# k^T v as pairs of 64-row matmuls, with v cast whole, in a linear-attention and mixture-of-experts kernel

## The chip, the cores and the metric

The kernel runs on one core of one Trainium2 chip. The metric is the device time of one execution in microseconds (us); less is better. "Span" is the time from the first to the last instruction of the profiled execution; it is about 1.8 us shorter than the device time of the same execution. Engines: PE (TensorE matmul), PEld (its weight loads), DVE (VectorE), ACT (ScalarE), POOL (GpSimd), SP (SyncE, which here only starts loads).

## The reference

Linear attention over q, k, v of 8 batches x 8 heads x 576 positions x 64, then a mixture of 8 experts in which every token goes through every expert, weighted by eight Sinkhorn rounds:

```python
q_p, k_p = phi(q), phi(k)                       # phi(x) = elu(x) + 1
kv  = np.einsum('bhsd,bhse->bhde', k_p, v)      # k^T v: what the change is about
z   = np.sum(k_p, axis=2)
num = np.einsum('bhsd,bhde->bhse', q_p, kv)
den = np.einsum('bhsd,bhd->bhs', q_p, z)[..., None] + 1e-06
x   = num / den                                 # then 4608 tokens x 512
for e in range(8):                              # P: gate, exp, Sinkhorn
    out += P[:, e:e+1] * (np.maximum(x @ w1[e], 0) @ w2[e])
```

## The kernel before

The attention part works on 16 groups of four heads. A group's k, q and v stand on 128 partitions: two "hh" halves of 64 partitions each hold different heads and share the matmuls. For k^T v that would mix heads of both halves, so v was cast into a tile of twice the width in which each half's columns are zero on the other half's partitions. The zeros were set once; each group's cast (float32 to float16 on POOL) wrote the two halves separately:

```python
vv_t = [fp.tile([P, 2, NJ, 2, D + 1], FP16, ...) for i in range(2)]   # zeroed at the start; column D is 1 (for z)
for hh in range(2):
    def f_v(e, hh=hh):
        s = slice(64 * hh, 64 * hh + 64)
        copy(e, gvv["tile"][s, :, :, hh, 0:D], gin["v"]["tile"][s])   # 64 partitions, 1152 elements each
    tvv.append(fadd({"pool": 1.35, "dve": 0.75} if n < 2 else ("pool", 1.35), f_v, ...))

def f_kv(_):
    gkv["tile"] = aps.tile([P, 2, 2, D + 1], FP32, tag="att", name="kv_ps")
    for j in range(NJ):                                               # NJ = 9
        nc.tensor.matmul(gkv["tile"], lhsT=gt["k"]["tile"][:, j, :, :].rearrange("p r d -> p (r d)"),
                         rhs=gvv["tile"][:, :, j, :, :], start=(j == 0), stop=(j == NJ - 1))
for rr in range(2):
    def f_z(e, rr=rr):                                                # PSUM to SBUF: kvz
        s = slice(64 * rr, 64 * rr + 64)
        copy(e, gz["tile"][s, :, rr, :], gkv["tile"][s, rr, :, :])
```

phi of k and q costs DVE three passes over SBUF, and these matter later:

```python
nc.vector.tensor_scalar(out=o, in0=gin[nm]["tile"], scalar1=1.0, ..., op0=ALU.add)            # tk, tq (or on ACT)
nc.vector.tensor_scalar(out=ge["tile"], in0=ge["tile"], scalar1=1.0, ..., op0=ALU.min)        # ek, eq
nc.vector.tensor_tensor(out=o, in0=o, in1=ge["tile"], op=ALU.max)                             # tk, tq: two SBUF inputs
```

After kv come q transposes (qt), den, num, the division (rden, xn), transposes of x (xt), and then the experts' matmuls hq and ye. All attention results in PSUM share one pool of two buffers (tag "att"). The order of every engine's queue is not written by hand: a small list scheduler (`_Plan`) places each piece on its engine by assumed durations (the numbers in `fadd`), priorities and the two-deep pools. A changed duration or pool therefore changes every queue.

The softmax here doesn't subtract the row's maximum and nothing guards it: scores larger than these inputs give would overflow.

## Time and profile before

| | before |
|---|---|
| device time, median of 4 runs | 1053.62 us (1052.89 to 1054.81) |
| profiled span | 1053.3 us |
| PE busy in the span | 1012.7 us (96%) |
| first expert matmul (hq) starts | 44.08 us |
| last attention tile gone | about 168 us |
| POOL casts of v | 32, 40.2 us in all |

How to read it: PE is the bound from the moment it can start on hq, so the time is made of three things: when hq starts, how much PE work follows it, and how long PE stands idle after it. The lines are in the prediction.

### The profile page before, as it was taken

The numbers are of one execution on the slowest core, as the hardware profiler recorded it, in microseconds if no ns is written. First come the engines' busy times: TensorE is split into PE (matmuls) and PEld (weight loads), VectorE is DVE, ScalarE is ACT, GpSimd is POOL, SyncE is SP. The second block draws the span as 40 slices with busy tenths as digits, with TensorE's granted clock in tenths as the row PEclk, the third lists the DMA queues.
The fourth block names the chain that finished last, engine by engine and source line by source line (L and its number), as shares of the span: only waits on it lengthen the run. The fifth ranks groups of instructions, "written<-read, shape, count | busy, mean of one in ns | idle before, by whom it ended". The sixth has DMA issues, their size and how long they took to land.

```text
span 1053.3 us, 17028 instructions
## 1 busy us (share of the span) xinstructions
PE 1012.7 (96%) x7048; PEld 652.9 (62%) x7048; DVE 730.2 (69%) x1507; ACT 432.1 (41%) x693; POOL 54.8 (5%) x55
## 2 busy tenths in 40 slices
PE   2799999999999999999999999999999999999997
PEld 1455565456666666666666666666666666666664
DVE  6787876847666766667666766677666766666666
ACT  4666664453333333333333333333333333333331
POOL 3332310000000000000000000000000000000000
PEclk9999999999999999999999999999999999999999
DMA  9969600050001300050002200050003100014333
GB/s 270 326 193 248 198 6 2 1 81 2 1 1 26 56 1 1 1 81 1 1 1 41 41 1 1 1 81 1 1 1 49 32 2 1 1 28 89 83 82 81
DMA packets 31966, 55.63 MB, mean 53 GB/s; under 512 B 2704, under 2 KB 10896, under 8 KB 31888
## 3 DMA queue, kind: packets, MB, share of 16 engines
q1 hardware_dynamic: 18816, 37.76, 12.1%
q0 software_dynamic: 13072, 16.79, 9.9%
q8 instruction: 55, 0.90, 0.4%
q14 instruction: 23, 0.19, 0.1%
HBM read 61.88 MB, written 9.44 MB: 68 GB/s over the span
## 4 chain that ended last, share of the span: by engine, by line
PE 88%; DVE 7%; DMA 2%; ACT 1%; issue 1%; POOL 0%; SPq 0%; DVEq 0%; POOLq 0%; ACTq 0%
PE hq L467 45%; PE ye L576 36%; PE ye L497 4%; DMA vin<-in_v_dram 1%; DMA kin<-in_k_dram 1%; PE kv_ps L261 1%; DVE tk L239 1%; DVE xn L329 1%; DVE tq L239 1%; PE xt_ps L340 1%; PE qt_ps L286 1%; PE num_ps L324 0%; DVE ek L237 0%; DVE gs L389 0%; DVE kvz L195 0%
## 5 line engine op out<-in xcount | busy, mean ns | idle before, releaser
L471 ACT ACTIVATE h<-hq 128x512 f16<-128x512 f32 x576 | 343.4, 597 | 552.0 <-PE hq L467 551.8
L467 PE MATMUL hq<-xT,w 128*128 128x512 f16 x2304 | 556.2, 379 | 0.6 <-ACT h L471 0.6
L587 DVE SCALAR_TENSOR_TENSOR acc<-ye,P_sb,acc 128x256 f32<-128x256 f32 x882 | 396.7, 483 | 144.4 <-PE ye L576 144.4
L467 PEld LDWEIGHTS <-w 128*128 128x128 f16 x2304 | 223.9, 98 | 197.1 <-issue 1.9
L576 PEld LDWEIGHTS <-S 128*128 128x128 f16 x2016 | 197.0, 98 | 51.4 <-DVE S L550 2.2
L576 PE MATMUL ye<-T,S 128*128 128x256 f16 x1512 | 196.0, 273 | 1.2 <-DVE S L550 1.2
L576 PEld LDWEIGHTS <-h 128*128 128x128 f16 x1512 | 147.9, 98 | 58.1 <-ACT h L471 0.6
L550 DVE TENSOR_TENSOR S<-h 128x1024 f16<-128x1024 f16 x126 | 86.8, 689 | 115.4 <-ACT h L471 115.4
L576 PE MATMUL ye<-w,h 128*128 128x256 f16 x1008 | 130.8, 273 | 0.4 <-ACT h L471 0.4
L497 PE MATMUL ye<-w,h 128*128 128x512 f16 x288 | 69.7, 385 | 0.0
L576 PE MATMUL ye<-w,S 128*128 128x256 f16 x504 | 65.3, 273 | 0.2 <-DVE S L550 0.2
L576 PE MATMUL ye<-T,h 128*128 128x256 f16 x504 | 65.3, 273 | 0.1
L181 POOL DMA_DIRECT2D w<-in_moe_w_dram x16 | 13.3, 830 | 659.6 <-PE hq L467 624.3
L197 POOL CAST vv<-vin 64x1152 f16<-64x1152 f32 x32 | 40.2, 1257 | 98.7 <-PE kv_ps L261 49.5
L497 PEld LDWEIGHTS <-h 128*128 128x128 f16 x288 | 27.1, 100 | 27.5 <-issue 2.2
L550 DVE TENSOR_TENSOR S<-h,S 128x1024 f16<-128x1024 f16 x63 | 43.2, 686 | 0.0
L550 DVE TENSOR_TENSOR S<-S,h 128x1024 f16<-128x1024 f16 x63 | 42.9, 681 | 0.0
L261 PE MATMUL kv_ps<-vv,tk 128*128 128x260 f16 x144 | 22.5, 309 | 7.4 <-DVE qpT L195 5.0
L329 DVE TENSOR_TENSOR xn<-num_ps,rden 128x512 f16<-128x512 f32 (+1 forms) x48 | 26.5, 596 | 2.7 <-PE num_ps L324 1.9
L286 PE MATMUL qt_ps<-ident,tq 128*128 128x128 f16 x144 | 13.7, 235 | 14.1 <-DVE tq L239 11.0
L324 PE MATMUL num_ps<-kvz,qpT 128*128 128x128 f16 x160 | 16.0, 229 | 9.2 <-DVE xn L329 6.6
L226 ACT ACTIVATE ek<-kin 128x1152 f16<-128x1152 f32 x16 | 18.6, 1162 | 14.5 <-DMA kin<-in_k_dram 10.6
(60 smaller groups left out, 330.9 us busy)
## 6 DMA issues: line engine op xcount, KB each, us to landing
w<-in_moe_w_dram POOLq DMA_DIRECT2D x16, 1024.0 KB, 9.5
kin<-in_k_dram SPq DMA_DIRECT2D x16, 576.0 KB, 5.3
qin<-in_q_dram SPq DMA_DIRECT2D x16, 576.0 KB, 5.5
vin<-in_v_dram SPq DMA_DIRECT2D x16, 576.0 KB, 5.9
out_dram<-acc SPq DMA_DIRECT2D x72, 128.0 KB, 2.4
wg_sb<-in_moe_w_gate_dram POOLq DMA_DIRECT2D x1, 8.0 KB, 15.7
```

Source lines behind the costliest of these rows:

```text
L197: nc.gpsimd.tensor_copy(out=dst, in_=src)
L226: nc.scalar.activation(out=ge["tile"], in_=gin[nm]["tile"], func=AF.Exp)
L239: nc.vector.tensor_tensor(out=o, in0=o, in1=ge["tile"], op=ALU.max)
L261: nc.tensor.matmul(gkv["tile"], lhsT=gt["k"]["tile"][:, j, :, :].rearrange("p r d -> p (r d)"), rhs=gvv["tile"][:, :, j, :, :], start=(j = ...
L286: nc.tensor.transpose(gp["tile"][:, j - j0, :, :].rearrange("p h w -> p (h w)"), gt["q"]["tile"][:, j, :, :].rearrange("p r d -> p (r d)") ...
L329: nc.vector.tensor_tensor(out=gxn["tile"][:, i0:i1], in0=gn["tile"][:, 0:i1 - i0].rearrange("p i r h e -> p i (r h) e"), in1=grd["tile"][: ...
L467: nc.tensor.matmul(ghq["tile"], lhsT=gw1["tile"][:, c, ts(f, P)], rhs=xT[c][:, ds(512 * g, 512)], start=(c == 0), stop=(c == NDT - 1))
L471: nc.scalar.activation(out=gh["tile"][:, f, :], in_=ghq["tile"], func=AF.Relu)
L497: nc.tensor.matmul(gy[tt]["tile"], lhsT=gh["tile"][:, f, ds(P * tt, P)], rhs=gw2["tile"][:, f, :], start=(f == 0), stop=(f == NFT - 1))
L550: nc.vector.tensor_tensor(out=Sx[:, i], in0=a0, in1=a1, op=op)
L576: nc.tensor.matmul(g_["tile"][:, col, :], lhsT=lhs(kk), rhs=rhs(kk), start=(first and kk == 0), stop=(kk == 3), skip_group_check=True)
L587: nc.vector.scalar_tensor_tensor(out=dst, in0=g_["tile"][:, col, :], scalar=P_sb[:, gg, e:e + 1], in1=dst, op0=ALU.mult, op1=ALU.add)
```

## The change

The intent: multiply the two halves side by side on the two row halves of the PE array, each into its own PSUM bank, so that no zeros are needed. v is then cast once, whole, into a tile of half the width, and PE streams 130 columns per pair where it streamed 260. The rest follows: two "att" buffers at once per kv group, four smaller PSUM copies for two, smaller memsets, and a scheduler that can grant two buffers of one pool to one piece. The diff is abridged: it leaves out that repair of the scheduler and the dependencies that came with it (kv now waits for its kvz tile to be granted, the q transposes and num for the tiles that their results go into). They are a part of what is called "the order" below.

```diff
-    vv_t = [fp.tile([P, 2, NJ, 2, D + 1], FP16, ...
+    vv_t = [fp.tile([P, 2, NJ, D + 1], FP16, ...
...
-        for hh in range(2):
-            def f_v(e, hh=hh):
-                s = slice(64 * hh, 64 * hh + 64)
-                copy(e, gvv["tile"][s, :, :, hh, 0:D], gin["v"]["tile"][s])
-            tvv.append(fadd({"pool": 1.35, "dve": 0.75} if n < 2 else ("pool", 1.35), f_v, ...
+        def f_v(e):
+            copy(e, gvv["tile"][:, :, :, 0:D], gin["v"]["tile"])
+        tvv.append(fadd({"pool": 1.3, "dve": 0.75} if n < 2 else ("pool", 1.3), f_v, ...
-        gkv, gz = S_.grp(p_att), S_.grp(p_kvz)
+        gkv, gz = [S_.grp(p_att), S_.grp(p_att)], S_.grp(p_kvz)
...
-            gkv["tile"] = aps.tile([P, 2, 2, D + 1], FP32, tag="att", name="kv_ps")
+            for hh in range(2):
+                gkv[hh]["tile"] = aps.tile([P, 2, D + 1], FP32, tag="att", name=f"kv_ps{hh}")
             for j in range(NJ):
-                nc.tensor.matmul(gkv["tile"], lhsT=gt["k"]["tile"][:, j, :, :]...,
-                                 rhs=gvv["tile"][:, :, j, :, :], start=(j == 0), stop=(j == NJ - 1))
+                for hh in range(2):
+                    s = slice(64 * hh, 64 * hh + 64)
+                    nc.tensor.matmul(gkv[hh]["tile"], lhsT=gt["k"]["tile"][s, j, :, :]...,
+                                     rhs=gvv["tile"][s, :, j, :], start=(j == 0), stop=(j == NJ - 1))
...
-            tz.append(fadd({"dve": 0.29, "act": 0.3}, f_z, ...      # one copy per rr
+                tz.append(fadd({"dve": 0.22, "act": 0.24}, f_z, ... # one copy per hh and rr
...
-        nc.vector.memset(vv_t[i], 0.0)
-        for hh in range(2):
-            nc.vector.memset(vv_t[i][64 * hh:64 * hh + 64, :, :, hh, D], 1.0)
+        nc.vector.memset(vv_t[i][:, :, :, D], 1.0)
```

More of the change, by code (lines that the diff above doesn't have):

```diff
@@ L59, in slot @@
             r = t["ready"]
+            seen = {}
             for g in t["acq"]:
                 o, n = g["pool"]["order"], g["pool"]["n"]
-                if len(o) >= n:
-                    for u in o[len(o) - n]["users"]:
+                i = len(o) + seen.get(id(o), 0)
+                seen[id(o)] = i + 1 - len(o)
+                if i >= n:
+                    for u in o[i - n]["users"]:
                         d = self.t[u]["done"]
@@ L163 @@
     fp = front.enter_context(tc.tile_pool(name="fp", bufs=2))
-    vv_t = [fp.tile([P, 2, NJ, 2, D + 1], FP16, tag=f"vv{i}", name=f"vv{i}", bufs=1) for i in range(2)]
+    vv_t = [fp.tile([P, 2, NJ, D + 1], FP16, tag=f"vv{i}", name=f"vv{i}", bufs=1) for i in range(2)]
     kvz_t = [fp.tile([P, 2, 2, D + 1], FP16, tag=f"kvz{i}", name=f"kvz{i}", bufs=1) for i in range(2)]
@@ L249, in att @@
         ta = fadd(("none", 0.0), f_va, deps=[tin["v"]], acq=[gvv], prio=pr)
-        for hh in range(2):
-            def f_v(e, hh=hh):
-                s = slice(64 * hh, 64 * hh + 64)
-                copy(e, gvv["tile"][s, :, :, hh, 0:D], gin["v"]["tile"][s])
-            tvv.append(fadd({"pool": 1.35, "dve": 0.75} if n < 2 else ("pool", 1.35), f_v, deps=[ta, tin["v"]],
-                            use=[gvv, gin["v"]], prio=pr))
-        gkv, gz = S_.grp(p_att), S_.grp(p_kvz)
+        def f_v(e):
+            copy(e, gvv["tile"][:, :, :, 0:D], gin["v"]["tile"])
@@ L258, in f_kv @@
+        tvv.append(fadd({"pool": 1.3, "dve": 0.75} if n < 2 else ("pool", 1.3), f_v, deps=[ta, tin["v"]],
+                        use=[gvv, gin["v"]], prio=pr))
+        gkv, gz = [S_.grp(p_att), S_.grp(p_att)], S_.grp(p_kvz)
         def f_kv(_):
-            gkv["tile"] = aps.tile([P, 2, 2, D + 1], FP32, tag="att", name="kv_ps")
+            for hh in range(2):
+                gkv[hh]["tile"] = aps.tile([P, 2, D + 1], FP32, tag="att", name=f"kv_ps{hh}")
             for j in range(NJ):
-                nc.tensor.matmul(gkv["tile"], lhsT=gt["k"]["tile"][:, j, :, :].rearrange("p r d -> p (r d)"),
-                                 rhs=gvv["tile"][:, :, j, :, :], start=(j == 0), stop=(j == NJ - 1))
@@ L263, in att @@
-        tkv = fadd(("pe", 1.0), f_kv, deps=[tph["k"]] + tvv, acq=[gkv], use=[gvv, gt["k"]], prio=pr)
+                for hh in range(2):
+                    s = slice(64 * hh, 64 * hh + 64)
+                    nc.tensor.matmul(gkv[hh]["tile"], lhsT=gt["k"]["tile"][s, j, :, :].rearrange("p r d -> p (r d)"),
+                                     rhs=gvv["tile"][s, :, j, :], start=(j == 0), stop=(j == NJ - 1))
         def f_za(_):
             gz["tile"] = kvz_t[(len(p_kvz["order"]) - 1) % 2]
-        tza = fadd(("none", 0.0), f_za, deps=[tkv], acq=[gz], prio=pr)
+        tza = fadd(("none", 0.0), f_za, deps=[tph["k"]] + tvv, acq=[gz], prio=pr)
@@ L268, in att, with f_z @@
+        tkv = fadd(("pe", 0.6), f_kv, deps=[tph["k"], tza] + tvv, acq=gkv, use=[gvv, gt["k"]], prio=pr)
         tz = []
-        for rr in range(2):
-            def f_z(e, rr=rr):
-                s = slice(64 * rr, 64 * rr + 64)
-                copy(e, gz["tile"][s, :, rr, :], gkv["tile"][s, rr, :, :])
-            tz.append(fadd({"dve": 0.29, "act": 0.3}, f_z, deps=[tza], use=[gkv, gz], prio=pr))
+        for hh in range(2):
+            for rr in range(2):
+                def f_z(e, rr=rr, hh=hh):
+                    s = slice(64 * rr, 64 * rr + 64)
+                    copy(e, gz["tile"][s, hh, rr, :], gkv[hh]["tile"][s, rr, :])
+                tz.append(fadd({"dve": 0.22, "act": 0.24}, f_z, deps=[tza, tkv], use=[gkv[hh], gz], prio=pr))
@@ L290, in f_qc @@
                 copy(e, gq["tile"][:, :, j0:j1, :].rearrange("p h j w -> p j h w"), gp["tile"][:, 0:j1 - j0])
-            t1 = fadd(("pe", 0.06 * (j1 - j0)), f_qt, deps=[tph["q"]], acq=[gp], use=[gt["q"]], prio=pr)
+            t1 = fadd(("pe", 0.06 * (j1 - j0)), f_qt, deps=[tph["q"], tqa], acq=[gp], use=[gt["q"]], prio=pr)
             tq.append(fadd({"act": 0.12 + 0.113 * (j1 - j0), "dve": 0.2 + 0.057 * (j1 - j0)}, f_qc, deps=[t1, tqa],
@@ L331, in f_xn @@
                     in1=grd["tile"][:, i0:i1, :, None].broadcast_to([P, i1 - i0, 4, D]), op=ALU.mult)
-            t1 = fadd(("pe", 0.12 * (i1 - i0)), f_num, deps=[tden], acq=[gn], use=[gq, gz], prio=pr)
+            t1 = fadd(("pe", 0.12 * (i1 - i0)), f_num, deps=[tden, txa], acq=[gn], use=[gq, gz], prio=pr)
             txn.append(fadd(("dve", 0.1 + 0.28 * (i1 - i0)), f_xn, deps=[t1, trd, txa], use=[gn, grd, gxn], prio=pr))
```

## The prediction

> **What bounds the kernel now.** I read the page's engine shares and slices first, to see which engine the time belongs to and where it is free.
>
> ```profile
> PE 1012.7 (96%) x7048; PEld 652.9 (62%) x7048; DVE 730.2 (69%) x1507; ACT 432.1 (41%) x693; POOL 54.8 (5%) x55
> ...
> PE   2799999999999999999999999999999999999997
> ...
> PEclk9999999999999999999999999999999999999999
> ```
>
> PE is busy in every slice but the first two, about 26 us each. The kernel has a start without PE work, then one long PE-bound stretch. The change touches only the attention part, whose tiles are gone by about 168 us; all later experts are the same program. So I read the first 200 us by stretches (columns: stretch, its length, then busy time and count of PE, PEld, DVE, ACT, POOL, granted clock, DMA share, GB/s).
>
> ```profile
> 0.00:20.00 20.00, 4.03 (x32) 2.78 (x33) 12.54 (x23) 6.99 (x6) 6.47 (x12) 1.00 1.00 263
> 20.00:40.00 20.00, 10.17 (x74) 7.54 (x72) 14.78 (x27) 12.39 (x14) 8.98 (x8) 1.00 1.08 348
> 40.00:60.00 20.00, 18.60 (x149) 11.29 (x147) 16.12 (x31) 13.57 (x19) 4.92 (x5) 1.00 0.77 261
> ...
> 80.00:100.00 20.00, 18.00 (x163) 11.09 (x162) 15.91 (x30) 14.85 (x23) 6.29 (x5) 1.00 1.06 281
> ...
> 120.00:140.00 20.00, 19.14 (x163) 11.55 (x162) 17.40 (x35) 13.98 (x18) 4.88 (x4) 1.00 0.39 120
> ```
>
> PE is idle for 16 us of the first 20 and 10 of the next, while the DMA share is at 1.00. From 40 to 180 us (the rows not shown here included) its idle time sums to 6.9 us. There PE alternates attention work with the first expert's matmuls (hq, ye) as filler, and the filler does not run out: by the chain of waits expert 0 still has PE work at 225 us, long after the front is over. So after about 44 us, a microsecond less PE work is a microsecond less time, and before that the end is set by how soon the first hq matmul can start. The timeline shows what that start waits for:
>
> ```profile
> 16.42 2.13 PE L261 MATMUL kv_ps<-vv,tk 128*128 128x260 f16 x9 [4.24 <-DVE qpT L195]
> ...
> 30.24 5.45 POOL L197 CAST vv<-vin 64x1152 f16<-64x1152 f32 x4 [8.70 <-DMA vin<-in_v_dram]
> ...
> 33.30 2.11 PE L261 MATMUL kv_ps<-vv,tk 128*128 128x260 f16 x9 [2.04 <-POOL vv L197]
> ...
> 35.20 0.45 PE L301 MATMUL den_ps<-kvz,qpT 128*128 128x2 f16 x10
> ...
> 44.08 2.66 PE L467 MATMUL hq<-xT,w 128*128 128x512 f16 x8
> ```
>
> The kv matmul at 33.30 belongs to the third (batch, head group), counting from zero number 2. It stands in PE's in-order queue ahead of the den and num matmuls of number 1, which hq needs. So the third v load, landing at about 30.2, and two casts of it (2.7 us) hold up the second group, and with it hq at 44.08. The first kv, at 16.42, waited not for v but for both PSUM buffers to be emptied of the q transposes.
>
> Last, the cost of the operations that change, by shape, and the spacing of kv matmuls in a warm stretch:
>
> ```profile
> L197 POOL CAST vv<-vin 64x1152 f16<-64x1152 f32 x32 | 40.2, 1257 | 98.7 <-PE kv_ps L261 49.5 <-issue 25.0 <-DMA vin<-in_v_dram 23.1
> L261 PE MATMUL kv_ps<-vv,tk 128*128 128x260 f16 x144 | 22.5, 309 | 7.4 <-DVE qpT L195 5.0 <-POOL vv L197 2.0 <-DVE xn L329 0.2
> ...
> L195 DVE CAST kvz<-kv_ps 64x130 f16<-64x130 f32 x21 | 6.1, 291 | 5.8 <-PE kv_ps L261 3.1 <-ACT kvz L193 2.6
> ```
> ```profile
> 71.24 1.16 PE L261 MATMUL kv_ps<-vv,tk 128*128 128x260 f16 x9
> 72.24 0.41 PE L301 MATMUL den_ps<-kvz,qpT 128*128 128x2 f16 x10
> 72.50 0.81 PE L497 MATMUL ye<-w,h 128*128 128x512 f16 x3
> ```
>
> The nine kv matmuls start at 71.24 and the next group at 72.24: 1.00 us, or 111 ns each, though one "lasts" 272 ns. The other 161 ns are pipeline depth, overlapped by the next. The ten den matmuls with their ten weight loads take 0.26 us, 26 ns a pair: that is how little a load with a short matmul can cost.
>
> **What the Trainium skill says.** "TensorE: Matmul & The Clock Gate", Part 3 (packing small matmuls), says that matmuls on different row groups of the array run at the same time, with starts some 4 ns apart, and gives 3.07x for four tiles of 32 rows; its Part 1 gives 55.6 ns between warm matmuls of 128 columns. The trace agrees with the second (111 ns at 260 columns is the same rate); nothing in it uses row groups. "TensorEngine Tiling (Array Packing)", Key Properties, says that changing the tiling mode drains the engine; every matmul here is 128*128, so the trace cannot show it. The same page, Gotcha 1 (PSUM Pressure), says that row tiles must write to different banks. Hence the two tiles of the change.
>
> **The change part by part.**
>
> (a) kv matmuls. 9 of 260 columns become 9 pairs of 130 columns; the built program places them at rows 0 and 64 of the array. Side by side, a pair costs about 130/260 of 111 ns plus a few ns, say 58 ns (two loads at 26 ns fit beneath it), 0.52 us for nine. For the two mode changes around each group I add 0.10 us, an estimate between nothing and twice the 161 ns depth: 0.62 us against 1.00. Counted from the first hq, the old order has 12 kv groups to run (numbers 4 to 15), the new order has 14 (2 to 15), because it starts hq earlier in the sequence. 12 x 1.00 - 14 x 0.62 = 3.3 us saved. The new order has also one den (0.26 us) more and one q transpose group (0.50 us) less to do after that point: 3.5 us saved in all.
>
> (b) v cast. Two casts of 64 partitions, median 1.18 us, become one of 128 partitions with the same 1152 elements a partition. Partitions run side by side, so I take 1.2 us for it. POOL loses some 19 us of work, nearly all beside other work; on the path it counts once or twice at the start.
>
> (c) memsets. Two of 2.0 us on DVE fall away; DVE starts tk when k lands (5.5 us) instead of 7.3. Hidden: the next thing needed, the first v, lands at 11.7.
>
> (d) evacuation. Two copies of 130 elements become four of 65. From xn (686 ns at 512, 417 at 256 elements) an element costs DVE 1.05 ns, so a copy falls from 291 to about 223 ns: 4 x 0.22 - 2 x 0.28 = 0.3 us more per group, 5 us over 16, on DVE and ACT, which have 2.6 to 4.1 us free of each 20 (DVE). Off the path as long as PE has filler.
>
> (e) PSUM buffers. A kv group now takes both "att" buffers: it waits for both earlier users, and the next users wait for its copies. And the slot fix reorders every engine's queue.
>
> (f) the start, walked by the new queues with the old durations. kv 0 now stands first in PE's queue: v at 11.7 plus the cast makes it start at 12.9 instead of 16.42. But its copies stand on DVE and ACT behind work on the second k and q, which land at 15.2 and 17.0, so kvz is ready at about 18.4 and xn 0 ends at about 23.1 (old: 24.4). kv 1 follows at about 28.3, behind ACT's and DVE's work on the third q (landed 24.9). Its copies on ACT stand behind the exponential of the fourth k, which now lands after the third v, at about 29.5: ready at 31.2 to 31.5. Then den 1, num 1 after a q transpose copied on ACT (33.4), xn 1 until 37.3, transposes and two copies on ACT until 39.5, nine q transposes, hq at about 40. The old order had kv 2 in this path, the new one has not: about 4 us gained, with 2.5 us of doubt either way.
>
> Sum: 3.5 (PE work) + 4 (start) - 1 (more idle on PE from (d), (e)) = 6.5 us. 1054.1 - 6.5 = 1047.6 us.
>
> **The rivals.** First, the pairs do not overlap, or the drains eat the overlap: 18 x 57 ns = 1.03 us a group plus up to 0.3 us of drains. The 14 groups then cost 14.4 to 18.6 us against 12.0, and with the earlier start the time is 1053 to 1057. For it: the drain is stated, and the groups are short; against it: two banks, two row groups, loads of 26 ns.
>
> Second, the two PSUM buffers become the bound of the front: in 50 to 170 us PE's largest wait is already num waiting for xn, 4.3 us, which is such a buffer wait. If each of the 14 groups left 0.5 us idle on PE in its order, 7 us come back and the time is about 1054. Against it: PE's new queue still has one to three filler groups of 0.86 us between kv and den and between num pieces.
>
> Third, the start does not move, because it hangs on inputs that land at the same rate (DMA share 1.00): then only (a) is left, about 1052. And if the queue order fits the real landings better than I walked it, hq could start at 36: about 1044.
>
> **Range and chances.** Two sizes carry the result, each with a few us of doubt: the start (1.5 to 6.5 us gained) and the PE work with its stalls (3 us lost to 6 gained). I take 1040 to 1055 for 8 in 10. Two per cent is 21 us; the kv groups as a whole hold only 22.5 us of PE time, so faster by 2% needs a luck at the start that the loads don't allow, and slower by 2% needs a stall that repeats in every group. Chances 0.02, 0.95, 0.03.
>
> **What would show it.** A warm kv group of 18 matmuls should last about 0.6 us from its first start to the next group's; 1.0 or more shows the first rival. The casts should number 16 at about 1.2 us, the kvz copies 64 at about 0.22. First hq near 40 us. PE's idle time from 40 to 180 us near 8; 14 or more shows the second rival. The last stage, from the first matmul of the second expert's products to the end, should be as long as before; if it isn't, the reordering reached further than I think and the prediction is wrong for a reason not listed here.

## The result

| | before | after |
|---|---|---|
| median of 4 runs | 1053.62 us | 1044.38 us (1044.05 to 1045.43) |
| ratio | | 0.9913 (95%: 0.9896 to 0.9930) |
| profiled span | 1053.3 us | 1042.2 us |
| first hq | 44.08 us | 39.67 us |

A ratio is the mean time of one kernel's fast runs over that of the other's fast runs of the same rounds, so it is not quite the ratio of the medians quoted. The change saves 9.2 us, 0.9%: inside the predicted range and within 2%, and 2.7 us more than the predicted 6.5.

The page of the kernel after, its engine shares and slices (busy tenths in 40 slices of 26 us):

```profile
PE 1003.0 (96%) x7192; PEld 645.8 (62%) x7192; DVE 719.4 (69%) x1511; ACT 433.3 (42%) x717; POOL 42.2 (4%) x39
...
PE   2699999999999999999999999999999999999997
```

PE has 144 matmuls more and is busy for 9.7 us less, and the picture is the same: a start, then PE without a pause. POOL lost 12.6 us of busy time (its casts 18.4, while its DMA issues took 5.8 more). DVE lost 10.8, of which the smaller memsets are 4.2. The other 6 or so are strange, as DVE was given more instructions, not fewer. That is the thread to pull. The same stretches as in the prediction, kernel after:

```profile
0.00:20.00 20.00, 2.55 (x32) 2.14 (x32) 8.55 (x20) 7.89 (x8) 5.49 (x11) 1.00 1.00 265
20.00:40.00 20.00, 10.79 (x102) 8.69 (x103) 13.39 (x28) 12.93 (x16) 2.30 (x2) 1.00 1.08 354
40.00:60.00 20.00, 17.67 (x169) 10.13 (x168) 15.17 (x31) 12.28 (x23) 2.31 (x2) 1.00 0.65 198
...
80.00:100.00 20.00, 19.87 (x194) 11.53 (x193) 15.26 (x32) 15.81 (x26) 3.77 (x4) 1.00 1.02 281
...
120.00:140.00 20.00, 19.81 (x182) 11.28 (x181) 15.20 (x30) 15.80 (x27) 3.67 (x3) 1.00 0.47 147
```

In the stretch from 80 us PE stood idle for 2.0 us before and for 0.13 now; from 120 us, 0.9 and 0.19. Over 40 to 180 us its idle time falls from 6.9 to 3.3 us. The prediction had it rise by 1. The timeline of PE at the start, kernel after (start, duration, engine, line, instruction, count, and in brackets the idle time before it and what ended it):

```profile
12.66 1.16 PE L265 MATMUL kv_ps<-vv,tk 64*128 64x130 f16 x18 [12.66 <-POOL vv L200]
...
27.75 1.52 PE L265 MATMUL kv_ps<-vv,tk 64*128 64x130 f16 x18
...
39.67 1.25 PE L470 MATMUL hq<-xT,w 128*128 128x512 f16 x4
40.85 0.69 PE L265 MATMUL kv_ps<-vv,tk 64*128 64x130 f16 x18
```

The first kv starts at 12.66 (walked: 12.9), the second at 27.75 (28.3), hq at 39.67 (about 40), and the third kv now comes after hq. A warm kv group, kernel after, to be held against the 71.24 line of the prediction:

```profile
69.61 0.38 PE L470 MATMUL hq<-xT,w 128*128 128x512 f16 x1
69.92 0.69 PE L265 MATMUL kv_ps<-vv,tk 64*128 64x130 f16 x18
70.54 1.90 PE L500 MATMUL ye<-w,h 128*128 128x512 f16 x8
```

First start to the next group's is 0.62 us, which looks like the predicted 0.62. But the group also starts 0.31 us after the last hq, where two hq stand 0.216 apart. In single starts: the two matmuls of a pair begin 1 to 4 ns apart, pairs 57 to 58 ns apart; the first pair starts 312 ns after the last hq (96 more than between hq), and ye starts 149 ns after the last pair (92 more than a plain pair's 57). So a group costs 0.72 us of PE, of which 0.19, not 0.10, is the change into the two-row tiling and out of it.

The groups of the changed operations, kernel after (count | busy us, mean ns | idle before, and what ended it):

```profile
L200 POOL CAST vv<-vin 128x1152 f16<-128x1152 f32 x16 | 21.8, 1363 | 121.1 <-PE kv_ps L265 82.5
L265 PE MATMUL kv_ps<-vv,tk 64*128 64x130 f16 x288 | 12.3, 228 | 12.9 <-POOL vv L200 12.7
L198 DVE CAST kvz<-kv_ps 64x65 f16<-64x65 f32 x32 | 6.6, 222 | 22.1 <-ACT kvz L196 12.3
```

The cast has a median of 1.15 us for twice the partitions; the mean of 1.36 comes from three casts of 2.28 us.

### Where the 9 us come from

The kernel before, run again as an experiment (b_same below), is the cleaner partner, with a span of 1051.3 us: the first profile holds a drop of the clock that did not come again. Against it the span after is 9.06 us shorter:

| term | predicted | measured |
|---|---|---|
| hq starts earlier (43.72 to 39.67) | 4 | 4.05 |
| less PE work after it | 3.5 | 2.2 |
| PE waits less after it | -1 | 2.8 (what is left of 9.06; in the records, PE's idle time from the first hq to its last instruction falls from 9.2 to 6.85, 2.3 of it, and its busy time by 2.6) |
| sum | 6.5 | 9.06 |

PE work: 12 kv groups at 1.00 us are 12.03, 14 at 0.72 are 10.07, so 2.0 instead of the predicted 3.3; with the den (+0.26) and the q transposes (-0.5) that change sides, 2.2.

PE's waits from 40 to 240 us (total us, times, longest), the kernel before (b_same) and after:

```profile
PE num_ps L324 <- DVE xn L329: 5.0, 8, 1.1
PE kv_ps L261 <- DVE qpT L195: 0.7, 2, 0.6
```
```profile
PE num_ps L329 <- DVE rden L312: 1.2, 1, 1.2
PE ye L579 <- DVE S L553: 1.2, 1, 1.2
PE den_ps L306 <- ACT kvz L196: 0.7, 4, 0.2
PE num_ps L329 <- DVE xn L334: 0.7, 1, 0.7
```

Before, num waited eight times for xn, which DVE was late with. Those 5.0 us are nearly gone. The diff leaves xn itself alone, but it reorders every queue, so this pair of views alone does not say what removed the wait: in a_fullmm below, the new order has 0.7 for xn and 6.5 for rden, another result of DVE. Why was DVE late before? The timeline of all engines around one v cast, before, with the lines of POOL and DVE:

```profile
72.52 2.58 POOL L197 CAST vv<-vin 64x1152 f16<-64x1152 f32 x2 [7.75 <-issue]
...
73.60 0.46 DVE L237 TENSOR_SCALAR ek<-ek 128x1152 f16<-128x1152 f16 x1
...
74.17 1.54 DVE L239 TENSOR_TENSOR tk<-tk,ek 128x1152 f16<-128x1152 f16 x1
...
75.74 0.69 DVE L329 TENSOR_TENSOR xn<-num_ps,rden 128x512 f16<-128x512 f32 x1
```

The max tk<-tk,ek takes 1.54 us here. The same instruction takes 758 ns wherever POOL is not casting. It ends at 75.71, one usual length after the second cast lets go, and xn, which num's buffer waits for, comes behind it. The same meeting after:

```profile
98.57 2.28 POOL L200 CAST vv<-vin 128x1152 f16<-128x1152 f32 x1 [7.51 <-PE kv_ps L265]
...
98.72 0.74 DVE L235 TENSOR_SCALAR tk<-kin 128x1152 f16<-128x1152 f32 x1
...
99.39 0.45 DVE L240 TENSOR_SCALAR ek<-ek 128x1152 f16<-128x1152 f16 x1
...
99.87 1.58 DVE L242 TENSOR_TENSOR tk<-tk,ek 128x1152 f16<-128x1152 f16 x1
```

Here both sides pay: the cast, recorded from 98.57, needs 2.28 instead of 1.15 us while DVE's add and min run at their usual length, and then the max waits for the cast to be done. The add got its turn first although the cast is recorded 0.15 us ahead of it, so recorded times on POOL are only that exact.

The Trainium skill names this: "SBUF — State Buffer", section "SBUF: two separate sides", says that DVE and GpSimd share a pair of ports, that it is "an exclusive lock, not a bandwidth split", held for the whole instruction by whichever came first, and that a DVE instruction contends for it in a two-port mode, or with two SBUF inputs against a GpSimd instruction that reads SBUF, as the cast does. The trace agrees as far as it shows the lock; it does not show an instruction's mode. I took every add, min and max of phi whose duration is over 0.1 us above its usual one (755, 447 and 758 ns). Before (b_same) these are 19 instructions, delayed by 13.2 us together; after, 14 and 7.3 us. All 19, and 12 of the 14, began under a cast, and each of these ended at that cast's recorded end plus its own usual duration, less 0.13 to 0.16 us. A slower rate for both would not give a fixed sum. xn and kvz, whose input is PSUM, do not show it: DVE's kvz copies take 291 ns begun under a cast and 290 clear of one in b_same, 222 and 221 after.

So halving the number of POOL instructions, not their size, gave DVE back some 6 us over the attention part, an engine that was 79% to 87% busy from 80 to 140 us while PE waited for it. This was read off the traces; the experiments test it.

### The profile page after: what moved, and what is told of

It reads as the page before. It is cut to its first block, busy times and chain, and to the rows that moved or that the text cites. A ratio compares the mean times of both kernels' runs of the same rounds, so it can differ in the third digit from the quotient of the medians.

```text
span 1042.2 us, 17323 instructions
## 1 busy us (share of the span) xinstructions
PE 1003.0 (96%) x7192; PEld 645.8 (62%) x7192; DVE 719.4 (69%) x1511; ACT 433.3 (42%) x717; POOL 42.2 (4%) x39
## 4 chain that ended last, share of the span: by engine, by line
PE 86%; issue 6%; DMA 4%; DVE 2%; ACT 0%; SPq 0%; POOL 0%; DVEq 0%; ACTq 0%; POOLq 0%
PE hq L470 44%; PE ye L579 36%; PE ye L500 3%; DMA vin<-in_v_dram 1%; DMA w<-in_moe_w_dram 1%; DMA qin<-in_q_dram 1%; PE kv_ps L265 1%; PE xt_ps L345 1%; PE qt_ps L291 1%; PE num_ps L329 1%; DVE acc L590 0%; DVE xn L334 0%; PE den_ps L306 0%; SPq L220 0%; DVE kvz L198 0%
## 5 line engine op out<-in xcount | busy, mean ns | idle before, releaser
L184 POOL DMA_DIRECT2D w<-in_moe_w_dram x16 | 19.1, 1193 | 638.8 <-PE hq L470 603.4
L200 POOL CAST vv<-vin 128x1152 f16<-128x1152 f32 x16 | 21.8, 1363 | 121.1 <-PE kv_ps L265 82.5
L265 PE MATMUL kv_ps<-vv,tk 64*128 64x130 f16 x288 | 12.3, 228 | 12.9 <-POOL vv L200 12.7
L198 DVE CAST kvz<-kv_ps 64x65 f16<-64x65 f32 x32 | 6.6, 222 | 22.1 <-ACT kvz L196 12.3
```

What stands on the lines that cost most here:

```text
L184: nc.gpsimd.dma_start(out=g["tile"], in_=AP(tensor=ten.tensor, offset=e * DM * F, ap=ap))
L200: nc.gpsimd.tensor_copy(out=dst, in_=src)
L265: nc.tensor.matmul(gkv[hh]["tile"], lhsT=gt["k"]["tile"][s, j, :, :].rearrange("p r d -> p (r d)"), rhs=gvv["tile"][s, :, j, :], start=(j ...
```

## The experiments

Twelve kernels ran, each beside runs of the kernel before. "b_" starts from the kernel before, "a_" and "v_" from the kernel after. All computed the right result except b_onecast.

### b_same: the kernel before, unchanged

No edit. The first profile of the kernel before has PE's clock falling for some 3 us after 108 logits matmuls of 8 columns in a row; is that a part of the cost?

> The kernel before, unchanged, for a second profile of it. In its first profile the granted clock fell to about 0.5 from 168.7 to 171.7 us, right after 108 logits matmuls of 8 columns in a row, which made eight ye matmuls last 380 to 427 ns instead of 216: 1.6 us in all. Theory: the burst of tiny matmuls causes it, so this profile shows the same drop at the same place. Rival: it is a chance event of that one run, and this profile has none. Time the same as before, ratio 1.000 +- 0.002, either way.

Measured: 1054.18 us, ratio 1.0002 (0.9989 to 1.0014), span 1051.3. The stretches (length, PE busy, granted clock, DMA share, GB/s), with PE alone for the second; first profile of before, all columns:

```profile
168.00:170.00 2.00, 2.00 (x39) 1.17 (x36) 0.93 (x4) 0.45 (x2) 0.00 (x0) 0.64 0.04 8
170.00:172.00 2.00, 2.00 (x6) 0.71 (x5) 1.37 (x3) 0.00 (x0) 0.00 (x0) 0.51 0.00 0
```

and b_same:

```profile
168.00:172.00 4.00, 4.00 (x37) 1.00 0.02 4
```

The drop (to 0.51, eight ye matmuls at 380 to 427 ns instead of 216, 1.6 us) did not come again after the same burst, so the theory is refuted. What did cause it is not shown. It is not counted as a gain of the change: that is why b_same is the partner in the account above.

### a_serial: the two halves one after the other

```diff
-            for j in range(NJ):
-                for hh in range(2):
+            for hh in range(2):
+                for j in range(NJ):
```

> The changed kernel with the nine matmuls of rows 0 to 63 first and the nine of rows 64 to 127 after them, instead of in pairs; every queue is otherwise in the same order. Theory: the pairs run side by side (starts 3 to 4 ns apart in the changed kernel's profile), so without pairing a group takes 18 x 56 = 1.0 us between its borders instead of 0.52, and 14 groups after the first hq cost 14 x 0.5 = 7 us: about 1051. Rival: the gain came from the new order of the queues alone and the filler absorbs the rest: within 1.5 us of 1044.4.

Measured: 1047.09 us, ratio 0.9942 (0.9928 to 0.9955), 2.7 us slower than the change. Less than half of the loss I expected, for two reasons. The group, kernel a_serial:

```profile
71.31 1.00 PE L265 MATMUL kv_ps<-vv,tk 64*128 64x130 f16 x18
72.24 1.90 PE L500 MATMUL ye<-w,h 128*128 128x512 f16 x8
```

It takes 780 ns from first to last start, against 475 for pairs, where eighteen in a row at 57 ns would take 970. The single starts show why: the first half's last matmul (the one that signals its buffer) starts at 71.786, but the second half's first (the one that waits for its own buffer) at 71.622, and four of nine starts of each half interleave. So even unpaired, the halves run into each other. 14 groups times 0.305 us are 4.3 us. The other reason: some 1.7 us came back, as PE stood idle for less behind the longer group (5.0 us after the first hq for 6.85): den's wait for kvz is gone (0.7 us) and num's for rden falls from 1.2 to 0.5. So the overlap is real, and the part of it that a_serial loses is 4.3 us of PE work; a full lack of it could not be had this way.

### a_switch2: one full-array matmul in the middle of each group

```diff
+                    if j == 4 and hh == 0:      # 128 rows, 2 columns, into spare columns of the same bank
+                        nc.tensor.matmul(gkv[0]["tile"][:, 2, 0:2], lhsT=ident, rhs=ident[:, 0:2], ...)
```

> The changed kernel with one full-array matmul of 2 columns put into the middle of each group of pairs, into unused columns of the first bank (result unused). In the changed kernel's profile a group has 96 ns extra at its first matmul and 92 ns extra after its last. Theory: each is the price of one change between full and half-row tiling, so the inserted matmul costs two more changes and its own 26 ns: 0.21 us for each of 14 groups, 3.0 us, about 1047.4. Rival: the extra at the borders comes from semaphores or from the change of PSUM bank, and the inserted matmul costs only 26 to 60 ns a group: at most 0.9 us, about 1045.

Measured: 1047.36 us, ratio 0.9942 (0.9930 to 0.9955), 3.0 us slower than the change, as the theory said. The group, kernel a_switch2:

```profile
70.69 0.40 PE L268 MATMUL kv_ps<-vv,tk 64*128 64x130 f16 x8
71.03 0.18 PE L266 MATMUL kv_ps<-ident 128*128 128x2 f16 x1
71.14 0.46 PE L268 MATMUL kv_ps<-vv,tk 64*128 64x130 f16 x10
```

It grew from 475 to 690 ns. Less 26 ns for a matmul that short (the den matmuls' spacing), two more changes of the tiling cost 189 ns, 95 each. The changed kernel pays two per group, 0.19 us.

### a_fullmm and a_twocasts: the change, one part at a time

a_fullmm keeps the change's scheduler, two buffers and four copies, but goes back to masked v, its memsets, nine full matmuls and two casts in one piece; a_twocasts only cuts the cast in two.

```diff
 # a_twocasts (a_fullmm has it too, with the masked tile)
-            copy(e, gvv["tile"][:, :, :, 0:D], gin["v"]["tile"])
+            for hh in range(2):
+                s = slice(64 * hh, 64 * hh + 64)
+                copy(e, gvv["tile"][s, :, :, 0:D], gin["v"]["tile"][s])
```
```diff
 # a_fullmm besides
-                for hh in range(2): ... nc.tensor.matmul(gkv[hh]["tile"], lhsT=...[s, j], rhs=...[s, :, j, :], ...)
+                nc.tensor.matmul(gkv[0]["tile"], lhsT=...[:, j], rhs=gvv["tile"][:, :, j, :, :], ...)
+            nc.tensor.matmul(gkv[1]["tile"][:, 0, 0, 0:2], lhsT=ident, rhs=ident[:, 0:2], start=True, stop=True)
```

> The changed kernel's plan (its order of the queues, two PSUM tiles held, four copies of 65) but with the old masked v of twice the width and nine full-array matmuls of 260 columns (one matmul of 2 columns writes the second tile). Theory: the earlier first hq, near 40 us, comes from the order, not from the cheaper operations, so it stays; each of 14 groups takes 1.0 us plus 0.03 instead of 0.72, 4.3 us more: about 1048.5 to 1049. Rival: the start came earlier because of the cheaper cast and matmuls, and then first hq moves back to 43 us or later and the time to 1052 or more.

> The changed kernel with v cast by two instructions of 64 partitions, one after the other, instead of one of 128; all queues in the same order. In the profiles so far a DVE maximum over two SBUF tiles takes 758 ns when no GpSimd cast runs and about 1550 when one does; the excess of the DVE operations of the front that overlap a cast sums to some 14 us in the kernel before, 7 in the changed one. Theory: the 16 extra casts slow DVE by 7 us or more in the front, its results come later than the plan thought, and PE waits more: 2 to 6 us slower than the changed kernel, 1046.5 to 1050. Rival (as the prediction had it): GpSimd's work lies beside other work and costs nothing: within 1 us of 1044.4.

Measured: a_fullmm 1057.86 us, ratio 1.0042 (1.0029 to 1.0054); a_twocasts 1050.23 us, ratio 0.9968 (0.9956 to 0.9981). Together with the change they make a ladder; each step is the difference of two ratios (each known to about 0.0013, 1.4 us) times 1053.6 us:

| step | ratio | us |
|---|---|---|
| before to a_fullmm: order, two buffers, four copies | 1.0000 to 1.0042 | +4.4 |
| to a_twocasts: pairs on the halves | to 0.9968 | -7.8 |
| to after: one cast for two | to 0.9913 | -5.8 |

The first hq stands at 39.97 us in a_fullmm, so the earlier start comes with the order alone, and yet that kernel is slower than before, and some 9 us over what was expected of it (1048.5 to 1049): the expectation counted PE's work alone, and in the new order DVE collides more (25 delayed instructions, 18.1 us). PE's waits from 40 to 240 us, kernel a_fullmm:

```profile
PE num_ps L330 <- DVE rden L313: 6.5, 11, 1.8
PE den_ps L307 <- ACT kvz L196: 2.4, 11, 0.3
```

The pairs then give more than their 4.3 us of PE work (14 x (1.00 - 0.72), and 0.4 for the extra two-column matmul); the rest I put down to the shorter way from kv to its copies (den's wait for kvz falls from 2.4 to 0.7 us), without a run of its own. For the last step, PE's waits in a_twocasts, from 40 to 240 us:

```profile
PE num_ps L331 <- DVE rden L314: 5.0, 8, 1.9
PE ye L581 <- DVE S L555: 1.2, 1, 1.2
```

A wait of eight times 0.6 us, as before the change, is back; in this order num stands for rden and no longer for xn, but either is DVE being late. PE runs the same instructions as in the kernel after; 23 DVE instructions are delayed by 16.3 us instead of 14 by 7.3.

### b_onecast: the kernel before without its second cast

```diff
-                copy(e, gvv["tile"][s, :, :, hh, 0:D], gin["v"]["tile"][s])
+                if hh == 0:
+                    copy(e, gvv["tile"][s, :, :, hh, 0:D], gin["v"]["tile"][s])
```

Half of v is missing, so the result is wrong (relative error 0.65). The scheduler is told nothing, so all queues stand as before.

> The kernel before with the second of its two casts of v left out (wrong result on purpose: half of the heads get v = 0); plan and queues in the same order. Theory: as for the run with two casts, turned round: DVE loses some 7 us less to overlapped casts, and PE's waits for xn (5.0 us in the second profile of before) fall by half or more: 2 to 4 us faster than before, about 1051. Rival: same time as before, 1053.9 within 1 us.

Measured: 1044.63 us, ratio 0.9915 (0.9900 to 0.9930): 8.8 us faster than before, as much as the whole change, without a single row-tiled matmul, and over twice the 2 to 4 us expected. Groups by shape from 40 to 180 us, before (count | busy us, mean ns | idle before):

```profile
L239 DVE TENSOR_TENSOR tk<-tk,ek 128x1152 f16<-128x1152 f16 x12 | 13.9, 1155 | 1.0
...
L237 DVE TENSOR_SCALAR ek<-ek 128x1152 f16<-128x1152 f16 x12 | 7.9, 659 | 0.2
```

and b_onecast:

```profile
L239 DVE TENSOR_TENSOR tk<-tk,ek 128x1152 f16<-128x1152 f16 x11 | 8.3, 758 | 0.9
...
L237 DVE TENSOR_SCALAR ek<-ek 128x1152 f16<-128x1152 f16 x11 | 5.6, 508 | 0.2
```

The max is at its bare 758 ns in the mean. Six delayed instructions are left, 3.6 us. PE's wait of num for xn falls from 5.0 to 0.7:

```profile
PE num_ps L325 <- DVE xn L330: 0.7, 2, 0.4
```

PE's idle time after the first hq goes from 9.2 to 3.4 us; hq starts 1.0 us earlier (42.7). Those two make 6.8 of the 8.3 us between the two spans; the other 1.5 us are less busy time of PE in the records and stay unexplained. The half that is missing changes values only; every matmul still runs.

### a_dummycast: a second POOL cast that nobody reads

Fewer casts could also help because v is ready earlier. The traces already speak against it beyond the start: in b_same, from group 4 on, kv starts 8 to 19 us after its last cast has ended. To test it, the change got back a second instruction of the same size, from a constant to a scratch tile, behind the real one.

```diff
             copy(e, gvv["tile"][:, :, :, 0:D], gin["v"]["tile"])
+            nc.gpsimd.tensor_copy(out=scr, in_=ones_t[:, None, :].broadcast_to([P, 9, 128]))
```

> The changed kernel with a second GpSimd instruction after each v cast, of the same size (128 x 1152, fp32 to fp16), which reads a constant and writes a scratch tile that nobody reads: kv does not wait for it. It tells apart the two ways in which the second cast of the run with two casts can have cost 5.9 us. Theory (DVE is slowed by overlapped GpSimd work on SBUF): 1048 to 1051, with the DVE excess back at 12 us or more. Rival (v was ready later and kv with it): within 1 us of 1044.4.

Measured: 1050.55 us, ratio 0.9979 (0.9965 to 0.9993), 6.2 us slower than the change and the same as a_twocasts. Groups by shape from 40 to 180 us, kernel a_dummycast:

```profile
L256 POOL CAST scr<-ones_t 128x1152 f16<-128x1152 f32 x12 | 19.5, 1627 | 0.0
...
L241 DVE TENSOR_SCALAR ek<-ek 128x1152 f16<-128x1152 f16 x12 | 11.9, 994 | 0.0
```

No one waits for scr, and from group 2 on kv starts 12 us or more after the cast of its v. So the cost is what the second cast does to DVE, not a later v: ek's mean is 994 ns against 488 in the change, and 23 instructions are delayed by 15.8 us.

### v_act: the casts on ACT instead

```diff
-        tvv.append(fadd({"pool": 1.3, "dve": 0.75} if n < 2 else ("pool", 1.3), f_v, ...
+        tvv.append(fadd({"pool": 1.3, "dve": 0.75} if n < 2 else ("act", 1.17), f_v, ...
```

> A version meant to be better: the changed kernel with the v casts of groups 2 to 15 on ACT (1.17 us each) instead of GpSimd, replanned. Theory: the remaining 7 us of DVE excess go, ACT has 4 to 5 us free of each 20 in the front and takes 1.17 of each 9.7, and PE waits less: 1041 to 1044. Rival: ACT becomes the engine that the relu and the copies wait for, and the time is 1045 or more.

Measured: 1062.13 us, ratio 1.0087 (1.0072 to 1.0101), which the rival (1045 or more) covers, but for another reason than ACT's load. One delayed DVE instruction was left (0.5 us), so the collisions are gone. But in the new plan ACT stood 6.41 us for a q to land, with tq, the cast of v and the copy of x^T behind it in that order. ACT and PE, kernel v_act:

```profile
39.56 1.16 ACT L229 ACTIVATE eq<-qin 128x1152 f16<-128x1152 f32 x1 [6.41 <-DMA qin<-in_q_dram]
41.68 1.14 ACT L196 CAST vv<-vin 128x1152 f16<-128x1152 f32 x1
42.72 0.63 ACT L196 COPY xT<-xt_ps 128x576 f16<-128x576 f16 x1
...
43.40 0.69 PE L345 MATMUL xt_ps<-ident,xn 128*128 128x128 f16 x5 [7.17 <-ACT xT L196]
46.98 1.91 PE L470 MATMUL hq<-xT,w 128*128 128x512 f16 x4
```

hq came 7.3 us later than in the change; the cast itself takes 1.1 us of the 7.17 that PE waited. A second loss lies at 246 us, where PE stood 6.06 us for acc, as DVE before it had waited 7.1 us for a weight load to land. So this run does not say what a cast on ACT is worth by itself, only that a new plan can put something urgent behind a late input.

### b_kv2late: the start alone, in the kernel before

The kv of group 2 is told to wait for group 1's x transposes, with everything else as before:

```diff
-        tkv = fadd(("pe", 1.0), f_kv, deps=[tph["k"]] + tvv, ...
+        tkv = fadd(("pe", 1.0), f_kv, deps=[tph["k"]] + tvv + (xt_last if n == 2 else []), ...
```

> The kernel before with one dependency added to its plan: the kv matmuls of group 2 come after the x transposes of group 1. Theory: the first hq waited for group 2's v only because of PE's queue order; with it mended first hq comes at 39 to 41.5 us instead of 43.7 to 44.1, with no row tiling and no whole cast, and the time falls by 2 to 4 us, to about 1051 (the later order of the queues changes too, which is worth a few us either way). Rival: the start is set by the loads and the casts, and first hq stays at 43 or later.

Measured: 1051.99 us, ratio 0.9983 (0.9970 to 0.9997). That is a little less than the 2 to 4 us expected. The first hq stands at 40.31 us, so the prediction's reason for the late start (kv of number 2 in the queue ahead of den and num of number 1) is shown. But 3.4 us of start gave some 1.5 to 2 us of time: PE's idle time after the first hq rose from 9.2 us in b_same to 10.0, with new waits (hq for h 1.5, num for rden 0.9) beside num's 4.3 for xn. And its busy time rose by 1.7, most of it in a stretch of low granted clock. From 48 to 50 us, b_kv2late and then b_same (length, busy of PE, PEld, DVE, ACT, POOL, granted clock, DMA share, GB/s):

```profile
48.00:50.00 2.00, 2.00 (x9) 0.97 (x8) 0.87 (x3) 1.76 (x2) 0.00 (x0) 0.50 0.68 257
```
```profile
48.00:50.00 2.00, 2.00 (x19) 1.29 (x19) 1.42 (x4) 1.49 (x2) 0.00 (x0) 1.00 0.84 304
```

There four hq last 631 ns instead of 379. Summed over neighbouring matmuls of one shape, at least 1.2 us went that way after the first hq, against 0.2 in b_same.

### v_wlate and v_wx18: the first expert's weights later

The start hangs on loads, at a DMA share of 1.00. Expert 0's weights share it with k, q and v. "after" is the scheduler's earliest time for w1 and w2:

```diff
-    w_t = {0: load_w1(0, prio=-300.0) + load_w2(0, prio=-250.0, after=4.0)}
+    w_t = {0: load_w1(0, prio=-300.0, after=7.2) + load_w2(0, prio=-250.0, after=10.4)}   # v_wlate
+    w_t = {0: load_w1(0, prio=-300.0, after=7.2) + load_w2(0, prio=-250.0, after=18.0)}   # v_wx18
```

> A version meant to be better: the changed kernel with the two weight loads of expert 0 moved on GpSimd's queue behind the first and second v cast; PE, DVE and ACT queues in the same order. Theory: in the first 40 us the DMA share is 1.0 and 2 x 2.1 MB of weights compete with the first k, q, v loads; at some 300 GB/s that is 14 us of traffic, so the second and third group's inputs land several us earlier and first hq moves from 39.7 to 33 to 37: 3 to 6 us faster, 1038 to 1041. Rival: the weights then land too late for hq or ye, or the later groups' loads wait instead, and the time stays within 1.5 us of 1044.4.

> The changed kernel with expert 0's first weight load behind the first v cast and its second behind the fourth; PE queue in the same order. With the second load behind the second cast, groups 0 and 1 came 3 to 5 us earlier, but the DVE queue then stood at the fourth q, which landed at 32 to 33 us as before, and first hq moved only from 39.7 to 39.1. Theory: without the 2.1 MB of the second load in the first 30 us the fourth q lands some 6 us earlier, first hq comes at 33 to 36 us, and the time falls by 3 to 6 us to 1038.5 to 1041.5. Rival: the ye matmuls then wait for the late weights, or other waits take it back: within 1.5 us of 1044.4.

Measured: v_wlate 1044.15 us, ratio 0.9912 (0.9898 to 0.9925), v_wx18 1043.78 us, ratio 0.9915 (0.9901 to 0.9929): both the same as the change. In v_wlate groups 0 and 1 were some 4 us earlier, but DVE then stood 4.2 us at the fourth q, which landed as late as ever (DVE's add on it starts at 32.30), and hq started at 39.06. In v_wx18 hq did start at 33.90, 5.8 us earlier; then DVE stood 6.5 us for a later q until 41.12, and num 3.9 us for rden behind it. Right after that wait the granted clock was 0.51 (44 to 48 us); counted as in b_kv2late, the low clock took at least 2.7 us after the first hq, against 0.2 in the change. The bytes before the last q are the same, so what was won at the front was given back behind it, in waits and in clock. The rival was right both times.

### v_rate: a plan with the real rate of the loads

The scheduler assumes 1.05 us of queue and 2.6 us of latency per load; the traces show loads landing much further apart. Told 2.0 and 3.5, with w1 and w2 later still, it puts the first eight hq directly behind groups 0 and 1:

```diff
-            tin[nm] = fadd(("sp", 1.05), fn, acq=[gr], prio=pr, lat=2.6)
+            tin[nm] = fadd(("sp", 2.0), fn, acq=[gr], prio=pr, lat=3.5)
...
-    w_t = {0: load_w1(0, prio=-300.0) + load_w2(0, prio=-250.0, after=4.0)}
+    w_t = {0: load_w1(0, prio=-300.0, after=11.0) + load_w2(0, prio=-250.0, after=23.5)}
```

> The changed kernel planned with the rate at which its inputs really land (2.0 us between loads of 0.59 MB and 3.5 us to landing, where the plan had 1.05 and 2.6), and with expert 0's weights behind the first and third v cast. In its order no engine stands at the third or fourth group's inputs before the first hq, and no reciprocal of a group stands behind a q that lands later. Theory: the start was held by queues that were planned for loads twice as fast; first hq comes at 27 to 31 us, and since the earlier filler is then followed by no long wait, 4 to 8 us of it are kept: 1036 to 1040. Rival: inputs and weights are bound by the load rate as a whole, and the time goes to later waits as it did with the two later weight loads: within 1.5 us of 1044.4, or slower.

Measured: 1040.38 us (1039.93 to 1040.71), ratio 0.9880 (0.9863 to 0.9896), at the edge of the expected 1036 to 1040: the best version, 12.5 us faster than before in the same rounds and 3.5 to 4 us faster than the change (by the ratios to before, 0.9880 and 0.9913, and by the medians). PE, kernel v_rate:

```profile
27.25 2.70 PE L470 MATMUL hq<-xT,w 128*128 128x512 f16 x8
...
40.94 1.86 PE L500 MATMUL ye<-w,h 128*128 128x512 f16 x4 [4.41 <-DMA w<-in_moe_w_dram]
```

hq starts 12.4 us earlier than in the change, and two thirds of that are lost again, 4.41 us of it at once: PE's filler ran out and it stood until w2 landed. After it the granted clock was 0.51 (42 to 46 us), and the low clock took at least 2.9 us after the first hq. The next step would be to find the w2 time between the two; it was not run.

## Why the prediction was right or wrong

The total was right (1044.38 in 1040 to 1055), but as a sum of one correct term and two errors that partly cancel, so hitting it this well was in part luck.

**(a) kv matmuls: mechanism right, one term too small.** Pairs overlap and cost 57 to 58 ns, as predicted (58). The step that was off is "for the two mode changes around each group I add 0.10 us": they measure 0.19 us (96 ns in, 92 out; a_switch2: 95 each). With 14 groups that is 1.3 us less saved, 2.2 instead of 3.5. The first rival (no overlap) is refuted by the pair starts and by a_serial.

**(b) v cast: the step that failed.** The cast's own time was right (1.15 us for 1.2). "POOL loses some 19 us of work, nearly all beside other work" was wrong in its second half: work on POOL is not beside work on DVE, it takes DVE's turn. Before, 19 instructions were held up by 13.2 us, and num's wait for xn (4.6 us from 40 to 240 us in the profile that the prediction read; 0.7 in b_onecast, where all queues stand as before) was largely the trace of it. The prediction saw that wait and booked it under the second rival, as a buffer wait that would grow. b_onecast (8.8 us from leaving out one cast), a_twocasts and a_dummycast (5.9 and 6.2 us from putting one back) show it in three ways. It could have been read before: the max tk<-tk,ek, one instruction of one shape, had a mean of 1107 ns over 16 where the undisturbed ones take 758, and the slow ones lay under casts.

**(c) memsets and (d) evacuation: right.** DVE starts tk at 4.73, off the path; the 64 copies take 222 ns on DVE (predicted 223) and 209 on ACT, and cause no wait beyond den's 0.7 us for kvz.

**(e) PSUM buffers: smaller than feared.** "-1 (more idle on PE from (d), (e))" was 2.8 us in the other direction. The new order does have a cost (a_fullmm, +4.4 us with its two casts), though most of the waiting there is for DVE's rden (6.5 us), and no run separates the buffers from it; the shorter kv and the single cast more than pay for it. The second rival is refuted: PE's idle time from 40 to 180 us is 3.3 us, not 14.

**(f) the start: right in each station.** 12.66, 27.75 and 39.67 us against 12.9, 28.3 and about 40; b_kv2late and a_fullmm show that the order, not the tiling, brings it. What the prediction took for granted, that a microsecond of start is a microsecond of time, is not general: b_kv2late kept about half of it, v_wx18 none of its 5.8 us and v_rate a third. In the change's own account it is a term of a sum whose parts were not run alone in that order.

**The tail** was as long as before: after 240 us PE is idle for 7.6 us in both. One new wait of 1.2 us (ye for S) came up between 220 and 240 us, from the reordering.

What stays open: how much of the 7.8 us step from a_fullmm to a_twocasts beyond 4.3 us is the shorter chain to kvz (den's wait falls by 1.7 us) and how much chance meetings of DVE and POOL in another order, as no kernel moved the one without the other. Open too is why b_kv2late, v_wx18 and v_rate keep just the share of their start that they keep: new waits and a low clock behind them are named above, but not undone one by one.

## What to carry to other kernels

An engine with much free time can still cost the bound engine time: before calling POOL work hidden, compare the durations of one and the same DVE instruction with and without a POOL instruction beside it, and count POOL instructions rather than their partitions. Row-tiled pairs halve the streaming time of a matmul, but each excursion costs about 0.19 us here and a pair saves 0.053 (111 - 58 ns), so by these numbers fewer than four such pairs in a run would not pay. An earlier start of the bound engine counts only as far as its inputs keep coming; in three versions here the wait behind it was followed by a granted clock of 0.50 or 0.51.

## What the Trainium skill lacked or had wrong

- "TensorEngine Tiling (Array Packing)", Key Properties, says that a change of the tiling mode drains the engine and gives no size. Here it costs 96 ns on the way in and 92 on the way out of a group, and 95 each in a_switch2.
- "TensorE: Matmul & The Clock Gate", Part 3 (packing small matmuls), says that matmuls on different row groups start some 4 ns apart (here 1 to 4 ns) and, under its mechanism, that matmuls start and end strictly in program order. In a_serial, whose source puts all nine matmuls of the first half ahead of the second half's, the second half's first starts at 71.622 us, 164 ns before the first half's last at 71.786. So on different row groups the starts did not keep the source's order; whether the built program does was not looked up.
- The same page's Part 1 ties a lower clock to idle time. In one profile of the kernel before, the clock fell to 0.51 at 170 us with PE busy in every record of the stretch, after 108 matmuls of 8 columns in a row, 25 ns apart; in a second profile of the same kernel it did not. The page has nothing on whether such a burst counts as busy, and no run here shows the cause.
- "SBUF — State Buffer" is right on the lock between VectorE and GpSimd; what it lacks is a size for the usual float16 passes. A 1152-element cast on POOL delayed a 758 ns max by about 0.8 us at each meeting, and two casts in place of one cost this kernel 5.8 us of 1044.
